# A gated long convolution beside a SiLU feed-forward on one core: another order of the seven products, constant matmuls at the start, an earlier load of S2, and a last product in two halves

## The chip, the core and the metric

The kernel runs on one core of a Trainium2 chip. The core has a matrix engine (TensorE, PE in the profile; its weight loads are PEld), VectorE (DVE), ScalarE (ACT), GpSimd (POOL) and a queue engine, SyncE (SP), from which most DMAs are issued; POOL issues the DMAs that add into DRAM. The metric is device microseconds of one execution; smaller is better. The profile's span runs from the first to the last instruction of the program.

## What is computed

```
xn = layernorm(q)                                   # q, k, v: 2048 x 1024
A:  k_shift = causal depthwise conv of k, 4 taps
    kv = k_shift * v
    y  = causal depthwise conv of kv with ssm_k (2048 taps, by FFT) + kv * ssm_D
    A  = xn * y
B:  h  = silu(xn @ w1)                              # w1: 1024 x 3584
    B  = h @ w2                                     # w2: 3584 x 1024
out = q + A + B
```

Everything is float32 outside; each matrix operand is held as a high and a low half in 16-bit floats, and a product is three matmuls (high·high, low·high, high·low).

## The kernel before

**The work.** It is one long stream on TensorE. The first GEMM (xn @ w1) has 14 pairs of 128-column blocks of w1. Pairs 0 and 1 of the first half of the rows run plainly (`plain_unit`, L951). All others run as *units* (`units`, L982): a two-by-two block product by seven products of sums instead of eight, named P1 to P7 in `PRODUCTS`, each of 12 matmuls of 512 columns. The left factors (A11, A12, A22, S1 to S4) are sums of transposed rows of xn and lie in eight big SBUF tiles, `places`; `XPLACE` says which. The right factors (B11, T2, T3, B21, B22, T1, T4) are sums of blocks of w1 and lie in the ring `wo`. There are 26 units: 12 for the first half of the rows (sp 0), 14 for the second (sp 1). The second GEMM (h @ w2) runs plainly for most of the hidden columns (`feed_forward`, L1031), over column halves h, rows of 128 t and chunks c of w2; rows in one entry of `TOGETHER` share a pass over the chunks. For eight hidden blocks (`PAIRS`) it runs by the same seven products in eight units (`units2`, L1092). Between these, the convolution (`convolution`, L1350) goes on mainly on VectorE, and its matmuls (L1520 to L1522 and L1711 to L1713) are put in between those of the GEMMs.

**A unit.** It holds three of the four PSUM banks of the ring `ff`: `one` (P1, then P2 added), `two` (a copy of P1, to which P6, P5 and P3 are added) and `c` (P7, then P4 added). The order on TensorE is P7, P6, P2, P5, then P1 of the *next* unit, then P3 and P4. `evacuate` (L909) is a stream of its own on ScalarE and VectorE: copy `one` into `two` after P1 (`seen["P1"]`, for which P6 waits); copy `two` to `u` after P6 (P5 waits for it); after P5 copy `two` to `d` (P3 waits for it); add `c` and `d` (P4 waits for it); SiLU of the sums. `evacuate2` (L1139) does the same in units2, with `a` in place of `u`, and its results are stored by POOL with an adding DMA (`G`), two of them through `copied`. Where a store is to be added to the last row block, the last unit first loads conv's part (`o`), adds it, and stores by SP (`L`). Buffers of these results come from `hfs`, six halves; `hts` holds the 16-bit halves of h and, later, parts of the convolution.

**The order of everything.** A planner (`Order`, L118) writes the order out when the program is built: each stream is a generator that yields operations (`Op`, with engine, reckoned duration, what it reads and writes) or waits for tokens; the planner always emits the operation with the smallest reckoned start less the stream's bias. The chip then runs each engine's instructions in that order, with semaphores in between. A change of an order or of a duration so re-plans all streams.

**The loads of the second half.** `load_x` (L1019) loads the seven sums of the second half from DRAM with transposing DMAs on SP, in the order of `PRODUCTS` (A11, S3, S2, A12, S1, S4, A22), each when the same place's sum of the first half has had its last use. Place 4 holds A21 first and then, as `room` (L861) says, the `parts` of the hidden quads in both halves; the chunks of w2 and the factors of units2 later take the places in the order of `W2PLACE` and `FPLACE`.

**The start.** `warm_up` (L1785) runs 22 matmuls of constants, 128x128 in float32 (two instructions each); the rows of x are then normalised, transposed on TensorE (L598) and split.

Of the kernel before, what the change touches and what calls it, by code (L numbers as in the profile page):

```python
# [11 lines left out]
F32 = mybir.dt.float32  # L12
# [6 lines left out]
ADD, SUB, MUL = ALU.add, ALU.subtract, ALU.mult  # L19

P = 128
# [96 lines left out]
class Order:  # L118
# [182 lines left out]
def h3_ffn_kernel(ctx, tc, x, kp, vs, fs, shift, dskip, w1, w2, cfwd, cinv, out):  # L301
# [559 lines left out]
    def room():  # L861

        for sp in range(2):
            yield flag["room", sp]
            yield places[4].ready
            t, tok = places[4].tile([P, 2, 2 * W], F32)
            parts.open(t, 2)
            yield flag["quads", sp]
            tok.set()
# [36 lines left out]
            add(blocks(i, b, hf, tok, (made,)), EB)  # L906
        return hf, made

    def evacuate(i, b, one, c, made, seen):  # L909

        yield ff.ready
        seen["bank"] = two, k2 = ff.tile([P, 4, P])
        yield a_act(two, one[0], AF.Copy)
        seen["P1"].set()
        yield vs_r.ready
        u, ut = vs_r.tile([P, 4, P])
        yield made["P6"]
# [9 lines left out]
        seen["P5"].set()  # L927
        low, done = yield from places_of(i, b + 1)
# [10 lines left out]
        add(silu(i, low, low, None, done), EB)  # L939

    def steps(o, w, xf, first, last, more=False):

# [39 lines left out]
    def units():  # L982

        todo = [(i, sp) for sp in range(2) for i in UNITS[sp]]
        yield ff.ready
        one = ff.tile([P, 4, P])
        yield from product("P1", *todo[0], one[0], True)
        for n, (i, sp) in enumerate(todo):
            if sp == 1:
                flag["unit", n - len(UNITS[0])].set()  # L990
                flag["room", 1].set()
            if i in PAIRS:
                add(quad(i, sp), 0.1)
            made, seen = defaultdict(Token), defaultdict(Token)
            yield ff.ready
            c = ff.tile([P, 4, P])
            add(evacuate(i, 2 * sp, one, c, made, seen), EB)
            yield from product("P7", i, sp, c[0], True)
            yield seen["P1"]
            two = seen["bank"][0]  # L1000
            yield from product("P6", i, sp, two)
            made["P6"].set()
            yield from product("P2", i, sp, one[0])
            made["P2"].set()
            yield seen["P6"]
            yield from product("P5", i, sp, two)
            made["P5"].set()
            if n + 1 < len(todo):
                yield ff.ready
                one = ff.tile([P, 4, P])  # L1010
# [5 lines left out]
            yield from product("P4", i, sp, c[0])  # L1016
# [14 lines left out]
    def feed_forward():  # L1031
# [13 lines left out]
        for h in range(2):  # L1045
            for ts in TOGETHER[h]:
# [17 lines left out]
        yield from units2()  # L1064


    TOGETHER = ([range(2)] + [(t,) for t in range(2, NT)],
                [(t,) for t in range(NT - 3)] + [range(NT - 3, NT)])

    def steps2(po, hx, wc, first, last, more=False):  # L1070
        for n in range(4):
            def mm(n=n):
                kw = dict(skip_group_check=more)
                nc.tensor.matmul(po, hx[:, n, 0, :], wc[:, n, 0, :], start=first and n == 0, stop=False, **kw)  # L1074
                nc.tensor.matmul(po, hx[:, n, 0, :], wc[:, n, 1, :], start=False, stop=False, **kw)  # L1075
                nc.tensor.matmul(po, hx[:, n, 1, :], wc[:, n, 0, :], start=False, stop=last and n == 3, **kw)  # L1076
            yield T(mm, po, [hx[:, n], wc[:, n]], 3 * 0.2185)

    tiles2 = [(sp, q) for sp in range(2) for q in range(4)]

    def uses2():

        yield 0, "P1"
        for u in range(len(tiles2)):
            for n in ("P7", "P6", "P2", "P5"):
                yield u, n
            if u + 1 < len(tiles2):
                yield u + 1, "P1"
            yield u, "P3"
            yield u, "P4"  # L1090

    def units2():  # L1092

        def product2(n, u, o, first=False):
# [4 lines left out]
            yield from steps2(o, hx, wc, first, True, not first)  # L1099
            htok.set()  # L1100
            if u == len(tiles2) - 1:
                wtok.set()

        yield ff.ready
        one = ff.tile([P, W])
        yield from product2("P1", 0, one[0], True)
        for u in range(len(tiles2)):
            made, seen = defaultdict(Token), defaultdict(Token)
            yield ff.ready
            c = ff.tile([P, W])  # L1110
            add(evacuate2(u, one, c, made, seen), EB)
            yield from product2("P7", u, c[0], True)
# [4 lines left out]
            yield from product2("P2", u, one[0])  # L1117
            made["P2"].set()
            yield seen["P6"]
            yield from product2("P5", u, two)  # L1120
            made["P5"].set()
            if u + 1 < len(tiles2):
                yield ff.ready
                one = ff.tile([P, W])
                yield from product2("P1", u + 1, one[0], True)
# [4 lines left out]
            yield from product2("P4", u, c[0])  # L1130
            made["P4"].set()

    def at(u, r, h):

# [1 line left out]
        t = 4 * (2 * sp + r) + q  # L1136
        return orr[t // T2, t % T2, :, h * W:(h + 1) * W]

    def evacuate2(u, one, c, made, seen):  # L1139
# [17 lines left out]
        yield made["P6"]  # L1157
        yield a_act(a, two, AF.Copy, invc2[:, 0:1])
        seen["P6"].set()
        yield made["P2"]  # L1160
        add(copied(*one, at(u, 0, 0)), EB)
# [4 lines left out]
        seen["P5"].set()  # L1166
        yield v_stt(d, c[0], invc2[:, 0:1], d, MUL, ADD)
        seen["P7"].set()
        yield G(at(u, 1, 1), d)
# [10 lines left out]
        yield made["P4"]  # L1180
        yield v_stt(a, c[0], invc2[:, 0:1], a, MUL, ADD)
# [603 lines left out]
    def warm_up():  # L1785
# [68 lines left out]
```

## Time and profile before

| what | us |
|---|---|
| median of three runs | 1257.39 (1256.72 to 1257.83) |
| the profiled execution | 1258.14 |
| its span, first to last instruction | 1256.4 |
| VectorE busy / ScalarE busy / POOL busy | 1117.9 / 790.5 / 83.5 |
| mean granted clock of TensorE, share of full | 0.994 |

The profiled execution is 0.75 us above the median of the runs, and 1.7 us of it lie outside the span. In the rows below a time is from the start of the span; a line of the timeline has start, duration, engine, line, operation, output and inputs, shapes, count, and in brackets how long the engine stood idle before it and what ended the wait. The records of successive matmuls overlap, so TensorE's pace is read from their starts or from their number in a window, not from their durations.

### The profile page before, as it was taken

The page shows a single profiled execution, that of the slowest core. Times are in us where ns is not written, and L with a number is a line of the kernel's source. Part 1 is how long each engine was busy: PE and PEld are TensorE (multiplying, and loading weights), DVE is VectorE, ACT ScalarE, POOL GpSimd, SP SyncE. Part 2 cuts the span into 40 slices and gives each one's busy share as a digit, 9 for nine tenths or more (in the row PEclk, how much of TensorE's full clock was granted, in tenths as well). Part 3 has the DMA queues.
Part 4 walks back from the last instruction along what each step waited for, and adds up shares of the span by engine and source line. Part 5 has one row for each costly group of instructions (what it writes and reads, how often), then busy time and mean ns, then how long its engine had stood idle before and what let it go on. Part 6 is the DMA issues. An engine that isn't in the chain of part 4 may idle for free. (4 is left out here: it accounts for less than half of the span.)

```text
span 1256.4 us, 17146 instructions
## 1 busy us (share of the span) xinstructions
PE 1232.6 (98%) x6034; PEld 597.5 (48%) x6034; DVE 1117.9 (89%) x1359; ACT 790.5 (63%) x1431; POOL 83.5 (7%) x93
## 2 busy tenths in 40 slices
PE   7999999999999999999999999999999999999996
PEld 6554444444444544444444544544544544454452
DVE  7999987997999789998999899799989889988970
ACT  7868888886588878568654643744653545563351
POOL 0000000000000000000000000000120030123132
PEclk8999999999999999999999999999999999999999
DMA  9276989989799899769984655688595497969765
GB/s 367 82 262 239 315 288 303 300 240 227 232 336 270 242 309 313 207 191 297 311 278 125 206 179 132 185 269 231 107 257 153 106 225 217 243 137 161 164 121 80
DMA packets 272662, 279.83 MB, mean 223 GB/s; under 512 B 73792, under 2 KB 192576, under 8 KB 271296
## 3 DMA queue, kind: packets, MB, share of 16 engines
q1 hardware_dynamic: 256848, 262.22, 67.9%
q0 software_dynamic: 15728, 16.52, 9.9%
q8 instruction: 47, 0.77, 0.3%
q14 instruction: 39, 0.32, 0.1%
HBM read 175.66 MB, written 88.34 MB: 210 GB/s over the span
## 5 line engine op out<-in xcount | busy, mean ns | idle before, releaser
L1074 PE MATMUL ff<-x,wo 128*128 128x512 f16 x864 | 327.9, 380 | 3.4 <-ACT hf L360 3.4
L1076 PE MATMUL ff<-x,wo 128*128 128x512 f16 x864 | 328.1, 380 | 0.0
L1075 PE MATMUL ff<-x,wo 128*128 128x512 f16 x864 | 327.9, 380 | 0.1
L946 PE MATMUL ff<-x,wo 128*128 128x512 f16 (+1 forms) x808 | 304.5, 377 | 6.2 <-ACT hf L360 3.0
L948 PE MATMUL ff<-x,wo 128*128 128x512 f16 (+1 forms) x808 | 304.8, 377 | 1.0 <-DVE wo L352 1.0
L947 PE MATMUL ff<-x,wo 128*128 128x512 f16 (+1 forms) x808 | 304.8, 377 | 0.0
L349 DVE TENSOR_TENSOR spec<-spec 128x512 f32<-128x512 f32 (+2 forms) x256 | 261.8, 1053 | 2.0
L1075 PEld LDWEIGHTS <-wo 128*128 128x128 f16 x864 | 84.6, 98 | 104.0 <-issue 4.7
L1076 PEld LDWEIGHTS <-wo 128*128 128x128 f16 x864 | 84.6, 98 | 102.6 <-issue 1.0
L1074 PEld LDWEIGHTS <-wo 128*128 128x128 f16 x864 | 85.5, 99 | 100.1 <-issue 0.6
L948 PEld LDWEIGHTS <-wo 128*128 128x128 f16 x808 | 79.6, 98 | 94.3 <-DVE wo L352 1.5
L947 PEld LDWEIGHTS <-wo 128*128 128x128 f16 x808 | 79.5, 98 | 93.8 <-issue 5.8
L946 PEld LDWEIGHTS <-wo 128*128 128x128 f16 x808 | 81.0, 100 | 90.2 <-ACT wo L360 1.7
L349 DVE TENSOR_TENSOR tmp<-spec 128x2048 f32<-128x2048 f32 (+1 forms) x48 | 92.7, 1933 | 0.9
L352 DVE SCALAR_TENSOR_TENSOR ht<-hf,wsc,ht 128x1024 f16<-128x1024 f32 (+1 forms) x56 | 67.4, 1203 | 7.5 <-ACT ht L360 7.2
L360 ACT ACTIVATE spec<-ps 128x512 f32<-128x512 f32 x92 | 53.2, 592 | 28.7 <-PE ps L1522 28.0
L352 DVE SCALAR_TENSOR_TENSOR wo<-raw,wsc,wo 128x512 f16<-128x512 f32 (+1 forms) x56 | 56.4, 1012 | 11.9 <-ACT wo L360 11.9
L346 POOL DMA_DIRECT2D out<-hf x47 | 45.8, 981 | 303.9 <-ACT hf L360 254.4
L360 ACT ACTIVATE hf<-ff,invc 128x512 f32<-128x512 f32 x32 | 21.9, 684 | 65.7 <-PE ff L1076 47.6
L360 ACT ACTIVATE ht<-hf,wsc 128x1024 f16<-128x1024 f32 (+1 forms) x56 | 60.8, 1085 | 3.4 <-DVE hf L349 2.1
L360 ACT ACTIVATE spec<-spec 128x1024 bf16<-128x1024 f32 x32 | 33.7, 1054 | 46.1 <-DVE spec L349 46.0
L349 DVE TENSOR_TENSOR spec<-tmp 128x512 f32<-128x512 f32 (+1 forms) x80 | 61.3, 792 | 0.7
(188 smaller groups left out, 1779.3 us busy)
## 6 DMA issues: line engine op xcount, KB each, us to landing
wo<-hs SPq DMA_DIRECT2D x160, 256.0 KB, 3.2
hs<-ht SPq DMA_DIRECT2D x80, 256.0 KB, 4.8
raw<-in_w SPq DMA_DIRECT2D x28, 512.0 KB, 5.9
wraw<-in_w SPq DMA_DIRECT2D x24, 512.0 KB, 5.4
w2n<-in_w SPq DMA_DIRECT2D x24, 512.0 KB, 6.1
out<-hf POOLq DMA_DIRECT2D x47, 256.0 KB, 4.5
kin<-in_kp SPq DMA_DIRECT2D x16, 704.0 KB, 5.1
xt<-in_x SPq DMA_DIRECT2D x16, 512.0 KB, 7.3
```

The costliest lines, as they stand in the source:

```text
L346: return Op("POOL", 1.1, 3.0, lambda: nc.gpsimd.dma_start(o, i, accum_op=ADD), [i], [o], m, 2.3 * n)
L349: return V(lambda: nc.vector.tensor_tensor(o, a, b, op=op), o, [a, b], **k)
L352: return V(lambda: nc.vector.scalar_tensor_tensor(o, a, s, b, op0=op0, op1=op1), o, [a, b] + ([] if isinstance(s, float) else [s]), **k)
L360: nc.scalar.activation(o, i, func, scale=scale, **kw)
L946: nc.tensor.matmul(o, w[:, 0, k], xf[:, :, k, 0], start=first and k == 0, stop=False, **kw)
L947: nc.tensor.matmul(o, w[:, 0, k], xf[:, :, k, 1], start=False, stop=False, **kw)
L948: nc.tensor.matmul(o, w[:, 1, k], xf[:, :, k, 0], start=False, stop=last and k == KH - 1, **kw)
L1074: nc.tensor.matmul(po, hx[:, n, 0, :], wc[:, n, 0, :], start=first and n == 0, stop=False, **kw)
L1075: nc.tensor.matmul(po, hx[:, n, 0, :], wc[:, n, 1, :], start=False, stop=False, **kw)
L1076: nc.tensor.matmul(po, hx[:, n, 1, :], wc[:, n, 0, :], start=False, stop=last and n == 3, **kw)
```

## The change

It has five parts.

1. In every unit but the first of `units` and the first of `units2` the products run P6, P7, P5, P2, next P1, P3, P4. With P1 the new `start` adds the unit's evacuation at once, ahead of the taking of a bank for `c`, which is taken when P7 begins. In `evacuate` the SiLU of P2's sum, and the buffer for it, come after P5's copy; the add of `c` and `d` is yielded only when P2 has been issued. In `evacuate2` P2's result is copied after the add of `c` and `d`.
2. `keep_warm` is a new stream with a bias of –0.3: wherever the planner would leave TensorE waiting by more than that, it puts constant matmuls of a reckoned 0.22 us, until row 3 of A12 is transposed. It holds one bank of `ff` so long.
3. `load_x` begins with S2, into place 4; the parts of the second half go to S2's old place. `W2PLACE` and `FPLACE` are rearranged.
4. The first pass of the second GEMM takes three row blocks together in place of two.
5. In the very last unit P4 runs by column halves, and each half is evacuated and stored by SP when it is done; P2's and P3's results and the buffer for conv's part may take a half of `hts`.

The diff, cut to its core:

```diff
-W2PLACE = [(2, 7, 6, 3, 4), (0, 1, 5, 2, 7)]
-FPLACE = (6, 3, 4, 0, 1, 5, 2, 7)
+W2PLACE = [(2, 4, 7, 0, 3), (1, 5, 6, 2, 4)]
+FPLACE = (7, 0, 3, 1, 5, 6, 2, 4)
...
-            yield places[4].ready
-            t, tok = places[4].tile([P, 2, 2 * W], F32)
+            r = places[(4, XPLACE["S2"])[sp]]
+            yield r.ready
+            t, tok = r.tile([P, 2, 2 * W], F32)
...
-    def evacuate(i, b, one, c, made, seen):
+    def evacuate(i, b, one, made, seen, early):
...
-        yield made["P2"]
-        up, both = yield from places_of(i, b)
-        add(silu(i, up[:, 0], *one, both), EB)
+        if early:
+            yield made["P2"]
+            yield from first()
         yield ws_r.ready
         d, dt = ws_r.tile([P, 4, P])
         yield made["P5"]
         yield a_act(d, two, AF.Copy)
         seen["P5"].set()
+        c = seen["c"]
+        if not early:
+            yield made["P2"]
+            yield from first()
...
+        def start(n):
+            i, sp = todo[n]
+            yield ff.ready
+            one = ff.tile([P, 4, P])
+            yield from product("P1", i, sp, one[0], True)
+            made, seen = defaultdict(Token), defaultdict(Token)
+            add(evacuate(i, 2 * sp, one, made, seen, n == 0), EB)
+            return one, made, seen
...
+            if n == 0:
+                yield from seventh()
             yield seen["P1"]
             two = seen["bank"][0]
             yield from product("P6", i, sp, two)
             made["P6"].set()
-            yield from product("P2", i, sp, one[0])
-            made["P2"].set()
+            yield from second() if n == 0 else seventh()
             yield seen["P6"]
             yield from product("P5", i, sp, two)
             made["P5"].set()
+            if n > 0:
+                yield from second()
             if n + 1 < len(todo):
-                yield ff.ready
-                one = ff.tile([P, 4, P])
-                yield from product("P1", *todo[n + 1], one[0], True)
+                following = yield from start(n + 1)
             yield seen["P5"]
             yield from product("P3", i, sp, two)
...
-        for name in [p[0] for p in PRODUCTS.values()]:
-            r = places[XPLACE[name]]
+        for name in ("S2", "A11", "S3", "S1", "A12", "S4", "A22"):
+            r = places[4 if name == "S2" else XPLACE[name]]
...
-    TOGETHER = ([range(2)] + [(t,) for t in range(2, NT)],
+    TOGETHER = ([range(3)] + [(t,) for t in range(3, NT)],
...
-            for n in ("P7", "P6", "P2", "P5"):
+            for n in ("P7", "P6", "P2", "P5") if u == 0 else ("P6", "P7", "P5", "P2"):
...
+            for q in range(2):
+                yield from product2("P4", u, seen["c"][0], cols=slice(q * W // 2, (q + 1) * W // 2), end=q == 1)
+                made["P4", q].set()
...
         def copied(src, tok, to):
-            yield hfs.ready
-            o, otok = hfs.tile([P, W])
+            yield lambda: hfs.ready() or last and hts.ready()
+            o, otok = (hfs if hfs.ready() else hts).tile([P, W])
...
         seen["P7"].set()
+        if u > 0:
+            yield made["P2"]
+            add(copied(*one, at(u, 0, 0)), EB)
         yield G(at(u, 1, 1), d)
         dt.set()
         if last:
             yield flag["conv out"]
-            yield hfs.ready
-            o, otok = hfs.tile([P, W])
+            yield lambda: hfs.ready() or hts.ready()
+            o, otok = (hfs if hfs.ready() else hts).tile([P, W])
...
+        for q in range(2):
+            yield made["P4", q]
+            cols = slice(q * W // 2, (q + 1) * W // 2)
+            yield v_stt(a[:, cols], c[0][:, cols], invc2[:, 0:1], a[:, cols], MUL, ADD)
+            yield L(at(u, 1, 0)[:, cols], a[:, cols])
         c[1].set()
-        yield L(at(u, 1, 0), a) if last else G(at(u, 1, 0), a)
         at_.set()
...
+    def keep_warm():
+
+        pt, tok = ff.tile([P, 4, P])
+        while not flag["turned", "A12", 3]():
+            yield T(lambda: nc.tensor.matmul(pt[:, 0, :], ones, ones, start=True, stop=True), pt[:, 0, :], [], 0.22)
+        tok.set()
...
+    add(keep_warm(), -0.3)
```

More of the change, by code (lines that the diff above doesn't have):

```diff
@@ L919, in evacuate, with first @@
         seen["P6"].set()
-        yield made["P2"]
-        up, both = yield from places_of(i, b)
-        add(silu(i, up[:, 0], *one, both), EB)
+        def first():
+            up, both = quads_up[i, b] = yield from places_of(i, b)
+            add(silu(i, up[:, 0], *one, both), EB)
+        if early:
+            yield made["P2"]
+            yield from first()
         yield ws_r.ready
@@ L939, in evacuate @@
         add(silu(i, low, low, None, done), EB)
+    quads_up = {}
     def steps(o, w, xf, first, last, more=False):
@@ L993, in units, with seventh, second @@
                 add(quad(i, sp), 0.1)
[L994 to L998, printed above, removed]
+            one, made, seen = following
+            def seventh():
+                yield ff.ready
+                seen["c"] = c = ff.tile([P, 4, P])
+                yield from product("P7", i, sp, c[0], True)
+            def second():
+                yield from product("P2", i, sp, one[0])
+                made["P2"].set()
+            if n == 0:
+                yield from seventh()
             yield seen["P1"]
@@ L1092, in units2, with product2 @@
     def units2():
-        def product2(n, u, o, first=False):
+        def product2(n, u, o, first=False, cols=slice(0, W), end=True):
             yield flag["h2", u, n]
@@ L1098, in product2, with start, seventh, second @@
             wc, wtok = w2f[n]
[L1099 to L1106, printed above, removed]
-        for u in range(len(tiles2)):
[L1108 to L1112, printed above, removed]
+            yield from steps2(o[:, cols], hx, wc[:, :, :, cols], first, True, not first)
+            if end:
+                htok.set()
+                if u == len(tiles2) - 1:
+                    wtok.set()
+        def start(u):
+            yield ff.ready
+            one = ff.tile([P, W])
+            yield from product2("P1", u, one[0], True)
+            made, seen = defaultdict(Token), defaultdict(Token)
+            add(evacuate2(u, one, made, seen), EB)
+            return one, made, seen
+        following = yield from start(0)
+        for u in range(len(tiles2)):
+            one, made, seen = following
+            def seventh():
+                yield ff.ready
+                seen["c"] = c = ff.tile([P, W])
+                yield from product2("P7", u, c[0], True)
+            def second():
+                yield from product2("P2", u, one[0])
+                made["P2"].set()
+            if u == 0:
+                yield from seventh()
             yield seen["P1"]
@@ L1116, in units2 @@
             made["P6"].set()
-            yield from product2("P2", u, one[0])
-            made["P2"].set()
+            yield from second() if u == 0 else seventh()
             yield seen["P6"]
@@ L1121, in units2 @@
             made["P5"].set()
+            if u > 0:
+                yield from second()
             if u + 1 < len(tiles2):
-                yield ff.ready
-                one = ff.tile([P, W])
-                yield from product2("P1", u + 1, one[0], True)
+                following = yield from start(u + 1)
             yield seen["P5"]
@@ L1166, in evacuate2 @@
         seen["P5"].set()
+        c = seen["c"]
         yield v_stt(d, c[0], invc2[:, 0:1], d, MUL, ADD)
         seen["P7"].set()
+        if u > 0:
+            yield made["P2"]
+            add(copied(*one, at(u, 0, 0)), EB)
         yield G(at(u, 1, 1), d)
```

29 lines of the change are left out of this document (17 added, 12 removed).

## The prediction

> **What bounds the kernel now.** I read the page's first two parts, then the matrix engine's waits. Columns of the waits: who waited for whom, microseconds in all, times, longest.
> ```profile
> span 1256.4 us, 17146 instructions
> ...
> PE 1232.6 (98%) x6034; PEld 597.5 (48%) x6034; DVE 1117.9 (89%) x1359; ACT 790.5 (63%) x1431; POOL 83.5 (7%) x93
> ...
> PE   7999999999999999999999999999999999999996
> ```
> ```profile
> PE ff L1074 <- ACT hf L360: 3.4, 2, 2.7
> PE ff L946 <- ACT hf L360: 3.0, 1, 3.0
> ...
> PE ff L946 <- DVE hf L349: 1.8, 1, 1.8
> ```
> The kernel is bound by TensorE: 98% busy, full in every slice but the first and the last. The change takes no product away, so it can only win what lies in the 24 us between 1232.6 and 1256.4, and in stretches where the clock is low. Two waits for ScalarE (3.0 in the FFN units, 3.4 in units2) and one for VectorE (1.8) are nearly all that is between the ends. VectorE at 89% is the next bound.
>
> The clock is read from windows laid on its changes. Columns: length, PE busy (x instructions), PEld, DVE, ACT, POOL, granted clock, DMA share, GB/s.
> ```profile
> 7.96:11.37 3.41, 1.48 (x14) 1.51 (x14) 2.61 (x6) 2.88 (x9) 0.00 (x0) 1.00 1.04 401
> 11.37:14.78 3.41, 1.09 (x9) 0.59 (x7) 3.23 (x12) 3.17 (x8) 0.00 (x0) 1.00 1.08 408
> 14.78:18.20 3.42, 2.45 (x12) 1.51 (x12) 3.42 (x8) 3.37 (x9) 0.00 (x0) 0.50 1.03 420
> 18.20:21.61 3.41, 3.41 (x18) 2.54 (x17) 3.27 (x10) 2.80 (x7) 0.00 (x0) 0.50 1.02 408
> 21.61:25.02 3.41, 3.41 (x33) 3.19 (x32) 1.62 (x5) 1.78 (x4) 0.00 (x0) 1.00 1.04 409
> ...
> 584.81:588.22 3.41, 0.45 (x4) 0.10 (x2) 2.77 (x5) 3.31 (x8) 0.00 (x0) 1.00 1.15 343
> 588.22:591.63 3.41, 3.41 (x10) 1.21 (x9) 3.38 (x4) 1.86 (x6) 0.00 (x0) 0.50 1.06 324
> ...
> 1236.76:1240.17 3.41, 1.14 (x6) 0.55 (x6) 0.00 (x0) 0.69 (x1) 0.00 (x0) 1.00 0.73 105
> 1240.17:1243.58 3.41, 3.06 (x8) 0.94 (x7) 0.00 (x0) 1.00 (x2) 0.86 (x1) 0.50 0.24 20
> ```
> Each window with 1.14 us or less of PE work in 3.41 is followed by half clock; the one with 1.48 is not. So a stall costs twice: itself, then half of what the next 3.41 us could do, up to 1.7 us.
>
> **Term A: constant matmuls at the start.**
> ```profile
> 16.07 0.40 PE L948 MATMUL ff<-x,wo 128*128 128x256 f16 x1 [0.97 <-DVE wo L352]
> ...
> 17.13 0.73 DVE L352 SCALAR_TENSOR_TENSOR wo<-x,wsc,wo 128x512 f16<-128x512 f32 x1
> ...
> 21.92 0.23 DVE L733 TENSOR_SCALAR wsc<-powers,pow 128x3 f32<-128x3 f32 x1
> ...
> 22.60 1.47 PE L598 MATMUL ft<-ident,xt 128*128 128x128 f32 x12
> ...
> 23.87 1.89 DVE L352 SCALAR_TENSOR_TENSOR x<-ft,x 128x512 f16<-128x512 f32 x3 [1.72 <-ACT x L360]
> ```
> keep_warm puts matmuls of constants into the waits ahead of the first products. The first products run at half clock until 21.61: 18 matmuls in a window where the next has 33. If the fillers raise the window 11.37–14.78 above 1.48, that goes. Not all is won, since the parts of W1 arrive when they arrive. At full clock a group of 12 takes 12 x 3.41/33 = 1.24 us. Group one runs from 16.07 to 17.3, group two waits for the part ready at 17.13 + 0.73 = 17.86, so groups two and three end at 20.3 where now they end at 22.60. The next rows' transposes come some 2 us earlier; their three splits on VectorE, now from 23.87 after 1.72 idle, can start when it comes free at 21.92 + 0.23 = 22.15, which is 1.7 earlier. From there both engines shift together. **A = 1.6**, between 0 (the clock falls all the same) and 3.4 (half of two windows). Fillers delay nothing if they stand only in reckoned waits; the PSUM bank they hold is given back when row 3 is transposed, ahead of the second unit.
>
> The Trainium skill, "TensorE: Matmul & The Clock Gate", section "Part 1: The HAM clock gate (the "warmup" mystery)", has the clock fall after at least one idle window of about 3.4 us. Here it fell after windows that held 0.45, 1.09 and 1.14 us of work, so the trace disagrees. By that rule B and C below would have no half-clock share, and the sum would be some 3 us smaller.
>
> **Term B: the last FFN unit.** Order before: P7, P6, P2, P5, next P1, P3, P4; the last unit has no next P1, so P3 follows P5 at once and waits for ScalarE's copy of P5's bank.
> ```profile
> 584.66 0.38 PE L948 MATMUL ff<-x,wo 128*128 128x512 f16 x1
> ...
> 587.37 0.58 ACT L360 ACTIVATE hf<-ff 128x512 f32<-128x512 f32 x1
> ```
> ```profile
> 588.00 0.40 PE L946 MATMUL ff<-x,wo 128*128 128x512 f16 x1 [2.96 <-ACT hf L360]
> ```
> ```profile
> 1244.00 0.38 PE L1074 MATMUL ff<-x,wo 128*128 128x512 f16 x1 [0.78 <-ACT hf L360]
> ...
> 1248.96 0.38 PE L1076 MATMUL ff<-x,wo 128*128 128x512 f16 x1
> ```
> Between 1244.00 and 1248.96 lie 23 steps of 0.216, so a product of 12 is 2.59 us. After the change P2 stands between P5 and P3 and covers 2.59 of the 588.00 – 584.66 – 0.22 = 3.12 lost; 0.53 is left, no window falls below 1.48, and the half-clock window (1.7) goes. **B = 3.12 + 1.7 – 0.53 = 4.3.** Upper end 4.8. Lower end 0, if ScalarE is later still by that much: its copy was itself held up by loads and conv work.
>
> **Term C: stalls of the last unit of units2.**
> ```profile
> 1226.05 0.69 ACT L360 ACTIVATE hf<-ff,invc 128x512 f32<-128x512 f32 x1 [3.62 <-PE ff L1076]
> ```
> ```profile
> 1234.09 1.77 POOL L346 DMA_DIRECT2D out<-hf  x2 [2.91 <-issue]
> ...
> 1235.99 0.38 PE L1076 MATMUL ff<-x,wo 128*128 128x512 f16 x1
> 1238.29 0.69 ACT L360 ACTIVATE hf<-ff,invc 128x512 f32<-128x512 f32 x1 [10.94 <-DMA out<-hf]
> 1239.03 0.38 PE L1074 MATMUL ff<-x,wo 128*128 128x512 f16 x1 [2.66 <-ACT hf L360]
> ...
> 1248.84 0.69 DVE L349 TENSOR_TENSOR hf<-hf 128x512 f32<-128x512 f32 x1 [4.11 <-DMA hf<-out]
> ...
> 1249.62 0.69 ACT L360 ACTIVATE hf<-ff,invc 128x512 f32<-128x512 f32 x1 [5.67 <-DVE hf L349]
> 1249.64 0.75 DVE L352 SCALAR_TENSOR_TENSOR hf<-ff,invc,hf 128x512 f32<-128x512 f32 x1
> 1250.42 0.34 SPq L336 DMA_DIRECT2D out<-hf  x1
> 1250.61 0.86 POOL L346 DMA_DIRECT2D out<-hf  x1 [4.60 <-ACT hf L360]
> ...
> DMA to landing us min/median/max: 2.0/4.1/5.7
> ```
> P3's wait at 1244.00 goes, with P2 between: 0.8, and its half-clock part makes it **1.2**. P5's wait at 1239.03 is another kind: the copy of P6 (1238.29) waited for a store out of its buffer. That store is the one of 1234.09, of what was copied at 1226.05, just ahead of this unit's first copy. The wait is 1239.03 – 1235.99 – 0.22 = 2.82, and with 1.2 of half clock 4.0. After the change the unit's first copy is issued right behind its P1, ahead of the previous unit's P3, so its buffer can only be one stored a product or two earlier; but P5 comes one product earlier too (P6, P7, P5). Upper end 4.0; lower end –2.6, if the landing stays where it is. I take **2.3**, nearer the upper end, because the late store can no longer be the buffer's last user.
>
> **Term D: the tail.** From the last matmul's start (1248.96) to the end of the last store (1250.61 + the median 4.1 = 1254.7) are 5.7 us; the span closes 1.7 later, as before. That store carries P3's bank: its copy (1249.62) waited for the buffer into which conv's part was read back, which was landed and added only at 1248.84 + 0.69. Now a free ht buffer may serve, so the copy starts when P3 ends, and the read-back on SP stands behind d's store as before, with all of P3 and P4 to land. Two halves of P4 are 24 matmuls at 3.41/33 = 0.10, as long as 12 at 0.216. P3's store lands at –2.6 + 0.4 + 0.7 + 0.3 + 4.1 = 2.9 after the last matmul's start; the second half of P4 at 0.3 + 0.4 (half of the 0.75) + 0.1 + 2.0 = 2.8. **D = 5.7 – 2.9 = 2.8**, between 1.0 (POOL's queue, which now takes d, P2's and P3's results within five us, is late by 1.8) and 3.2.
>
> **Term E: the early S2.** load_x is one sequence on SP's queue. Now S2 goes first, into place 4, which the last quad must free; A11 stands behind it, and the first P1 of the second half needs A11.
> ```profile
> L342 SPq DMA_TRANSPOSE x<-xspA x3: 4722/4793/4934, 273.7 to 309.7; - x3
> ...
> L352 DVE SCALAR_TENSOR_TENSOR ht<-x,wsc,ht x1: 1276/1276/1276, 273.1 to 273.1; 128x1024 f16<-128x1024 f32 x1
> ...
> DMA to landing us min/median/max: 6.8/7.4/9.2
> ```
> Place 4 is read until 273.1 + 1.3 = 274.4; S2's issue takes 4.8; A11 lands at 274.4 + 4.8 + 7.4 = 286.6, against 273.7 + 7.4 = 281.1 now. P1 of that unit stands behind four products with conv matmuls between, which can fill. **E = –0.5**, from 0 to –3.5 (landing 9.2, no conv to fill).
>
> **Term F: seams elsewhere.** P1 to P6 loses a product of cover (P3, P4, P7 becomes P3, P4, 5.2 us); P5 to P3 gains one; P6 to P5 keeps one. VectorE's add for P7 is now issued behind P2, and P4 waits for it over P1 and P3 as before; behind it on VectorE stand splits and conv. The written order re-plans every conv step. The 1.8 for VectorE may go or move. Bounds: +2 (it goes) and –13 (four stalls as dear as 588's with half clock would be 19, as dear as the plain ones 7; I take the middle). I take **–2**, near the plain row of 1.8. The places' new order follows the order in which products release them; the three rows at GEMM2's start give each chunk of W2 one product more cover: nothing.
>
> **Sum:** 1.6 + 4.3 + 1.2 + 2.3 + 2.8 – 0.5 – 2 = 9.7. The profiled execution took 1258.1 (span 1256.4 and 1.7 around it), so 1248.4; the median shown, 1257.4, is 0.7 under it, so **1247.7**.
>
> **Rivals.**
> 1. The fillers don't hold the clock (the planner sees too few waits): A = 0, **1249.3**, chance 0.15. For: it reckons 0.44 for each warm-up matmul, and those ended early. Against: 0.4 us more work lifts the window above 1.48. The Trainium skill, "TensorE: Matmul & The Clock Gate", section "Part 4: PE-mode transpose", says that transposes do not count as busy for the gate; then the window would need more fillers. Against that stands 7.96–11.37: nearly all of its 1.48 are transposes, and the next window has full clock.
> 2. The last unit's buffer still lands late and P5 comes a product sooner: C's second part –2.6 in place of 2.3, **1252.6**, chance 0.15. For: the 7 us between 1226.05 + 0.69 and the store's issue at 1234.09 are POOL's queue, which the change leaves full.
> 3. Seams give it back: two stalls like 588's (9.4), **1257**, chance 0.12: VectorE at 89% has little room when TensorE gains.
> 4. Slower: P1 to P6, at 5.2 us of cover. Where ScalarE also serves conv (290 to 597) it was behind by 587.37 – 584.88 = 2.5 us once; a silu and a copy must fit. Each miss costs 1.9 to 4.8; against the 11.7 gained without F it decides from about four misses on: **1261**, chance 0.16. Against: no wait of that place is among the rows.
>
> **How the numbers follow.** My forecast has 0.42. A measurement tells about 0.2% (2.5 us) from no change. Faster: 0.42 + 0.15 + 0.15 = 0.72; same 0.12; slower 0.16. The range, 1240 to 1258.5, reaches down to A, B, C and D at their upper ends less 2, and up over rival 3; it leaves out rival 4 and little below.
>
> **What would show it.** Right: no window at half clock between 14 and 22; no wait of P3 for ScalarE's copy of P5 in either last unit; last store landed about 2.9 after the last matmul's start. Wrong: new waits of PE for ACT or DVE at the head of a unit (P6), a gap in PE near 285 for A11, or P5 of the last unit still behind a store.

## The result and the profile after

The changed kernel takes 1257.55 us in the median of 12 runs (1253.22 to 1261.77); the kernel before took 1256.64 beside it (12 runs, 1254.72 to 1257.83). The ratio is 1.0004, with a 95% interval of 0.9992 to 1.0016: no difference. Forecast was 1247.7. The profiled execution of the changed kernel took 1256.67, of which 2.27 lie outside its span (before: 1.7). One execution among the runs below, of a_tail2, took 1685 us at a granted clock of 0.72 and is left out of that run's median and ratio.

The page's first parts, for the changed kernel:
```profile
span 1254.4 us, 17286 instructions
...
PE 1233.2 (98%) x6092; PEld 602.1 (48%) x6092; DVE 1116.4 (89%) x1360; ACT 788.5 (63%) x1431; POOL 83.4 (7%) x93
...
PE   9999999999999999999999999999999999999997
```
The first slice is full now, and the last one is at 7 tenths where it was at 6. The windows at the start (columns as in the prediction: length, PE, PEld, DVE, ACT, POOL, granted clock, DMA share, GB/s) and the last row transposes ahead of the first whole products:
```profile
11.37:14.78 3.41, 3.31 (x30) 3.13 (x29) 3.24 (x12) 3.16 (x8) 0.00 (x0) 1.00 1.07 403
14.78:18.20 3.42, 3.42 (x33) 3.20 (x32) 3.42 (x8) 3.39 (x9) 0.00 (x0) 1.00 1.03 414
18.20:21.61 3.41, 3.41 (x34) 3.19 (x33) 3.27 (x10) 3.26 (x8) 0.00 (x0) 1.00 1.04 418
```
```profile
42.74 1.82 PE L598 MATMUL ft<-ident,xt 128*128 128x128 f32 x12 [0.34 <-DVE x L352]
```
The same line in the kernel before:
```profile
44.65 1.82 PE L598 MATMUL ft<-ident,xt 128*128 128x128 f32 x12 [0.34 <-DVE x L352]
```
The constant matmuls keep the clock at full speed, and all that follows comes 1.91 us earlier: term A is there (1.6 was forecast). The waits of TensorE for others in the changed kernel (us in all, times, longest):
```profile
PE ff L958 <- ACT hf L360: 3.9, 4, 2.3
PE ps L1578 <- ACT tmp L360: 3.2, 2, 2.3
...
PE py L491 <- ACT spec L360: 0.6, 1, 0.6
```
The wait of the last FFN unit, both waits of units2's last unit and the 1.8 for VectorE are gone; in their place stand four waits of other FFN units for a copy by ScalarE and four of conv's matmuls (`ps`, `py`; the fourth, 0.4, for VectorE), which waited once before, for 0.6.

The head of P3 in the last FFN unit (its first matmul is the last line):
```profile
590.47 0.38 PE L960 MATMUL ff<-x,wo 128*128 128x512 f16 x1
590.90 0.38 PE L958 MATMUL ff<-x,wo 128*128 128x512 f16 x1
```
It loses 590.90 – 590.47 – 0.22 = 0.2 us, where it lost 3.1 and then 1.7 in a window of half clock: term B is 4.6 (4.3). The last unit of units2, from P5's copy to the end:
```profile
1237.82 0.69 ACT L360 ACTIVATE hf<-ff,invc 128x512 f32<-128x512 f32 x1 [4.64 <-DMA out<-hf]
...
1239.71 0.86 POOL L346 DMA_DIRECT2D out<-hf  x1 [6.24 <-DVE hf L352]
...
1243.81 0.33 SPq L336 DMA_DIRECT2D hf<-out  x1
...
1245.16 0.27 PE L1102 MATMUL ff<-x,wo 128*128 128x256 f16 x1
1247.08 0.69 DVE L349 TENSOR_TENSOR hf<-hf 128x512 f32<-128x512 f32 x1 [7.79 <-DMA hf<-out]
1247.86 0.69 ACT L360 ACTIVATE hf<-ff,invc 128x512 f32<-128x512 f32 x1 [6.91 <-DVE hf L349]
...
1248.39 0.81 SPq L336 DMA_DIRECT2D out<-hf  x2
1248.90 0.86 POOL L346 DMA_DIRECT2D out<-hf  x1 [6.78 <-ACT hf L360]
```
TensorE waits for nothing here (term C is 2.82 + 1.2 + 0.8 + 0.4 = 5.2, where 3.5 was forecast). P5's copy (1237.82) still stood behind a store out of its buffer, as its row says, but it starts 0.35 us after P5's end (last matmul at 1237.25, plus 0.22), and P2 covers that. TensorE starts its last matmul at 1245.16, 3.8 earlier than before. But the span ends 9.24 after that, not 7.44. The read-back of conv's part (1243.81) is issued 4.1 us after the store of P5's result (1239.71), and all behind it waits for it: the addition, the copy of P3's bank, the last store.

So the account of the two profiled executions is: start 1.9, last FFN unit 4.6, last unit of units2 5.2, together 11.7; but the last matmul is only 3.8 earlier, so **7.9 are lost between**; the tail loses 1.8 and what lies outside the span 0.5. That leaves 1.5 (1258.14 – 1256.67); the medians, which differ by nothing, lie 1 us above the one trace of the changed kernel and 1.5 under that of the kernel before. The 7.9 can also be added up from the trace: what the spacings of successive matmul starts have over 0.216 (512 columns; 0.109 for 256) comes to 9.9 us between 47 and 1245, against 12.1 before, of which B and C were 10.0. This sum is called the stream's loss below.

### The profile page after: what moved, and what is told of

The parts are those of the page before. It is cut to its first block, busy times and chain, and to the rows that moved or that the text cites. A ratio compares the mean times of both kernels' runs of the same rounds, so it can differ in the third digit from the quotient of the medians.

```text
span 1254.4 us, 17286 instructions
## 1 busy us (share of the span) xinstructions
PE 1233.2 (98%) x6092; PEld 602.1 (48%) x6092; DVE 1116.4 (89%) x1360; ACT 788.5 (63%) x1431; POOL 83.4 (7%) x93
## 4 chain that ended last, share of the span: by engine, by line
PE 72%; DVE 11%; DMA 7%; ACT 6%; issue 3%; SPq 0%; POOLq 0%; POOL 0%; DVEq 0%; ACTq 0%
PE ff L1100 12%; PE ff L1101 12%; PE ff L1102 12%; PE ff L958 9%; PE ff L959 9%; PE ff L960 9%; DVE spec L349 4%; DMA w2n<-in_w 2%; PE ps L1578 2%; DVE tmp L349 2%; PE ps L1580 2%; PE ps L1579 2%; DMA lo<-cm 1%; DVE x L352 1%; ACT hf L360 1%
## 5 line engine op out<-in xcount | busy, mean ns | idle before, releaser
L352 DVE SCALAR_TENSOR_TENSOR acc<-kin,taps,acc 128x1024 f32<-128x1024 f32 x48 | 61.5, 1281 | 1.5 <-ACT acc L360 1.5
```

Source lines behind the costliest of these rows:

```text
L352: return V(lambda: nc.vector.scalar_tensor_tensor(o, a, s, b, op0=op0, op1=op1), o, [a, b] + ([] if isinstance(s, float) else [s]), **k)
```

## Experiments

Two theories on the 7.9 us. **T2**, which I favoured: the new order puts P6 right behind the previous unit's P4, so ScalarE's copy of P6, for which P5 waits, stands in its queue behind that unit's SiLUs and splits. **T1**: VectorE is nearly as full as TensorE in the middle, with ScalarE in step with it, so time gained by TensorE comes back as waits, whatever the order. Columns as before, the changed kernel by stage:
```profile
290.00:600.00 310.00, 305.59 (x1469) 143.57 (x1468) 280.11 (x321) 235.43 (x411) 2.27 (x3) 1.00 0.87 261
600.00:900.00 300.00, 297.09 (x1444) 141.30 (x1443) 280.60 (x297) 153.14 (x307) 4.99 (x6) 1.00 0.69 208
900.00:1080.00 180.00, 179.96 (x874) 85.47 (x873) 167.21 (x184) 94.07 (x196) 29.29 (x30) 1.00 0.79 192
```
VectorE is busy 90, 94 and 93% there (the 99% of the first expectation below is too high). For T2 speaks the largest of the FFN units' waits; the rows are TensorE's last matmul of P6 and first of P5, and ScalarE's queue:
```profile
511.79 0.38 PE L960 MATMUL ff<-x,wo 128*128 128x512 f16 x1
514.50 0.38 PE L958 MATMUL ff<-x,wo 128*128 128x512 f16 x1 [2.33 <-ACT hf L360]
```
```profile
507.52 0.72 ACT L360 ACTIVATE cm<-acc,csc 128x512 f16<-128x512 f32 x1 [5.03 <-DMA lo<-cm]
508.15 0.67 ACT L360 ACTIVATE x<-ff,wsc 128x512 f32<-128x512 f32 x1
508.85 1.15 ACT L360 ACTIVATE ht<-x,wsc 128x1024 f16<-128x1024 f32 x1
...
512.06 1.15 ACT L360 ACTIVATE hf<-hf,wsc 128x1024 f32<-128x1024 f32 x1 [0.41 <-DVE hf L349]
513.24 0.72 ACT L360 ACTIVATE ht<-hf,wsc 128x512 f16<-128x512 f32 x1
513.87 0.58 ACT L360 ACTIVATE hf<-ff 128x512 f32<-128x512 f32 x1
```
The bank is complete at 511.79 + 0.22, the copy (513.87) starts 1.9 later, behind a SiLU (512.06) and a split. In the mean over the 26 units this lag, from the start of P6's last matmul plus 0.216 to the copy, is 1.53 us in the changed kernel and 0.45 in the kernel before.

Times are medians of 4 to 12 executions; the ratio is to the kernel before on the same chip (1256.3 to 1257.1 in all four groups).

| run | us | ratio (95%) |
|---|---|---|
| b_warm | 1252.76 | 0.9973 (0.9962 to 0.9984) |
| a_nowarm | 1255.31 | 0.9995 (0.9983 to 1.0007) |
| a_oldunits | 1250.29 | 0.9949 (0.9936 to 0.9961) |
| a_tail | 1251.34 | 0.9959 (0.9946 to 0.9972) |
| after2 | 1258.10 | 1.0016 (1.0003 to 1.0030) |
| a_ulow | 1255.88 | 0.9993 (0.9981 to 1.0006) |
| a_old_tail | 1248.87 | 0.9937 (0.9919 to 0.9954) |
| a_old2_tail | 1249.94 | 0.9949 (0.9932 to 0.9965) |
| a_oldunits2 | 1251.51 | 0.9960 (0.9945 to 0.9975) |
| a_old_tail2 | 1247.78 | 0.9928 (0.9911 to 0.9945) |
| b_warm_tail | 1250.96 | 0.9952 (0.9936 to 0.9968) |
| a_old_tail_whole | 1246.55 | 0.9918 (0.9901 to 0.9934) |
| a_tail2 | 1252.86 | 0.9968 (0.9958 to 0.9978) |
| a_ulow_tail | 1251.01 | 0.9955 (0.9942 to 0.9968) |
| best_nowarm | 1250.58 | 0.9947 (0.9936 to 0.9959) |
| best_lateS2 | 1248.47 | 0.9934 (0.9923 to 0.9946) |

The traces show which pairs have one order: where only the last unit's buffers differ, or only the halves of the last P4, or only the constant matmuls, TensorE, ScalarE and VectorE keep the order of all other instructions. Every other edit lets the planner rearrange conv's steps, so a part of its difference is the new plan.

### The constant matmuls

b_warm is the kernel before with this line and `keep_warm`; a_nowarm is the changed kernel without the line.
```diff
+    add(keep_warm(), -0.3)
```


> The kernel before with the constant matmuls ahead of the first products added, and nothing else. Theory T2 (the new order of the units loses time by itself, because ScalarE's copy of P6 now queues behind the previous unit's SiLUs): with the old order the start's gain has nobody to eat it, so 1.5 to 2 us less than before, about 1255. Theory T1 (VectorE, busy over 99% between 290 and 900, sets the pace in the middle, whatever the order): the first products end 1.9 us earlier, but new waits of TensorE for VectorE or ScalarE give it back by the start of the second GEMM, so 1256.6, the time of before, within 0.5.

> The changed kernel without the constant matmuls ahead of the first products. T2: the waits of P5 for the copy of P6 stay (some 4 us over the FFN's units), and the start's loss of 1.9 us is seen in full: about 1259.4. T1: the units begin 1.9 us later, the side engines are less behind, so some 2 us of TensorE's waits in the middle go: 1257.5, as the changed kernel.

In the old order they are worth 3.7 us (1252.76 against 1256.46), which T1 doesn't allow and which is more than the 1.9 of the start: in the profiled execution the stall at 585 is there with 2.67, but without the half clock behind it. In the new order they are worth nothing: a_nowarm is not slower than the changed kernel but 1 to 2.6 us faster by the ratios (the intervals overlap), as T1 has it. Since the orders are the same, this is no new plan: in a_nowarm's trace the row transposes shown above begin 1.73 us later (44.47), and the stream's loss behind them is 5.6 us where it is 9.9 and, in after2, 8.6. Neither theory holds alone.

### The order of the FFN units

```diff
-            add(evacuate(i, 2 * sp, one, made, seen, n == 0), EB)
+            add(evacuate(i, 2 * sp, one, made, seen, n + 1 < len(todo)), EB)
...
-            if n == 0:
+            if n + 1 < len(todo):
                 yield from seventh()
...
-            yield from second() if n == 0 else seventh()
+            yield from second() if n + 1 < len(todo) else seventh()
...
-            if n > 0:
+            if n + 1 == len(todo):
                 yield from second()
```


> The changed kernel with the order of before (P7, P6, P2, P5) in all units of the first GEMM pair but the last one; the second GEMM's order, the constant matmuls, the early S2 and the halves of the last P4 stay. T2: the lag from the end of P6 to the start of its copy falls from 1.5 us in the mean back to about 0.45, P5's waits for it go, and the time is 5 to 7 us under the changed kernel, about 1251. T1: the waits move to another product, or to the conv matmuls, and the time is 1256 to 1258.

> The changed kernel once more, beside the other three on the same chip, since single runs of it lay between 1253.2 and 1261.8. Both theories: 1257.5, within 1; the waits of P5 for the copy of P6 of units 12 to 23 are there again, some 3 to 5 us together, though not in the same units.

> The kernel with the old order in the first GEMM pair's units but the last, once more, beside the same with the other buffers, on one chip: the first time the two were 1.4 us apart (1250.29 and 1248.87) where the traces' tails differ by 4.3. If the tail's gain holds here too, this run is 3 to 5 us above the next one, near 1251; if not, within 2 us of it.

With the old order in all units but the last the kernel takes 1250.29 and 1251.51, where the changed kernel takes 1257.55 and 1258.10: about 7 us. The mean lag of the copy is 0.61 and 0.65. (after2 shows how much single traces differ: its FFN units wait once, for 1.5, where the first trace has 3.9.) The waits that are left, in a_oldunits2:
```profile
PE ff L958 <- ACT hf L360: 2.1, 2, 1.8
...
PE ps L1578 <- ACT tmp L360: 0.8, 1, 0.8
```
The 1.8 is the same P5 as at 514 above, and the order isn't its cause: ScalarE, which keeps its order, stood 3.47 us ahead of conv's `cm` for a transposing load, and the copy behind it.
```profile
512.72 0.72 ACT L360 ACTIVATE cm<-acc,csc 128x512 f16<-128x512 f32 x1 [3.47 <-DMA lo<-cm]
...
514.39 0.57 ACT L360 ACTIVATE hf<-ff 128x512 f32<-128x512 f32 x1
```

### The SiLU ahead of the copy

The new order stays; only the SiLU of a unit's low pair waits for the next unit's copy of P6.
```diff
...
+        if gate is not None:
+            yield gate
         yield a_act(o, src, AF.Silu, wsc[:, i, 3:4])
...
+        flag["u copied", n].set()
...
-        add(silu(i, low, low, None, done), EB)
+        add(silu(i, low, low, None, done, flag["u copied", n + 1] if n < 25 else None), EB)
```


> The changed kernel with its new order, in which only the SiLU of a unit's low pair (behind P4) is issued on ScalarE behind the next unit's copy of P6. T2 (the copy stands in ScalarE's queue behind that SiLU): the mean lag from P6's end to its copy falls from 1.5 us to under 0.8, P5's waits of units 12 to 23 mostly go, and the time is 3 to 5 us under the changed kernel, about 1253.5. T1 (VectorE sets the pace, the order doesn't matter): the waits come back at other products or at the conv matmuls, 1256 to 1258.

> The changed kernel with the last unit's buffers from the other pool, once more, as the base for the next one: 1251 to 1252.5.

> The same with the SiLU of a unit's low pair issued behind the next unit's copy of P6. T2 alone: all that the old order gains comes from ScalarE's queue at that place, so this one reaches the old order with these buffers: 1248 to 1249. T1 beside it: only a part comes back (without these buffers it was 2 us) and the rest is waits of TensorE in other places: 1250 to 1251.

The lag falls to 0.66 (0.57 in a_ulow_tail), and in a_ulow one wait of 0.1 is left of the FFN units' 3.9. Yet the time falls by 2.2 us only (1255.88 against 1258.10), and with the other buffers of the next section by 1.9 (1251.01 against 1252.86), in both pairs with overlapping intervals, where the old order brings about 7 and about 4 (2.5 and 5.1 in its two pairs). The waits of a_ulow:
```profile
PE ff L1107 <- DVE x L352: 1.9, 1, 1.9
...
PE ff L1106 <- ACT ff L360: 1.3, 1, 1.3
PE ps L1584 <- ACT tmp L360: 1.2, 1, 1.2
...
PE ff L1106 <- ACT x L360: 0.7, 1, 0.7
```
TensorE now waits in the second GEMM, between 1075 and 1096: for operands (`x`, 1.9 and 0.7), which VectorE and ScalarE make beside conv, and for a copy of P1 (`ff`, 1.3). The trace of a_ulow_tail has waits in the same place, the longest (2.3) followed by a window of half clock. **T2 as the only cause falls.** It accounts for about 2 us of the 4 to 7. That the rest is T1 is not shown, for conv's plan is another one too. The single traces speak for a larger part: the stream's loss is 8.6 to 14.3 us (11.4 in the mean) in the four traces of the new order with the constant matmuls, 6.2 and 8.5 with this SiLU moved, and 2.3 to 8.0 (5.7 in the mean) in the eight with the old order in all FFN units but the last. But a trace is one execution: that of a_ulow took 1253.14, 2.7 less than its median and no more than that of a_oldunits (1253.39).

### The tail's buffers

TensorE's order is that of the changed kernel.
```diff
-            o, otok = (hfs if hfs.ready() else hts).tile([P, W])
+            o, otok = (hts if last and hts.ready() else hfs).tile([P, W])
...
-            o, otok = (hfs if hfs.ready() else hts).tile([P, W])
+            o, otok = (hts if hts.ready() else hfs).tile([P, W])
             yield L(o, at(u, 1, 0))
```


> The changed kernel, in which in the last unit the buffer for the read-back of conv's part and those of the copies of P2 and P3 are taken from the other pool (ht) first, so that the read-back needn't wait for the store of P5's result. TensorE's order is the same. Tail theory (the end is a chain of latencies: store of d, read-back into the same half, add, copy of P3 into that half again, store): the read-back is issued about 4 us sooner, P3's copy starts when P3 ends, and the last store lands 3 to 4 us earlier: about 1254. Rival (the last stores wait for POOL's queue or for the DMA engines, not for the buffer): within 0.5 us of the changed kernel.

> The old order in all units of the first GEMM pair but the last, and the last unit's buffers from the other pool. If the two are independent, both gains add: 1250.3 less the tail's 4.3 (tail of 4.93 us in the trace of the run with the other buffers against 9.24) is 1246. If the tail's gain comes only where TensorE runs late (the store that it waits for is then already landed), it is 1249 to 1250.

> The best so far, once more, on the same chip as the one before: 1247 to 1249 by either reading; what is told apart is its distance from the one before.

> The kernel before with the constant matmuls and the last unit's buffers from the other pool; TensorE's order and all the rest as before. Tail theory: the store, read-back, add, copy and store stand in the kernel before as well, so the buffers alone give 2 to 4 us on the 1252.8 with the constant matmuls: 1249 to 1251. If it is as fast as the kernel with the last units' new order (1248.9), the new order of the last units, the early S2 and the halves are worth nothing beside the buffers; by the trace they should be worth 3 to 5 us (the waits at 585, 1233 and 1236 with the constant matmuls: 2.67, 1.78 and 0.78).

a_tail is 6.2 us faster than the changed kernel, a_tail2 5.2 than after2. With the old order the buffers bring 1.4 in the first pair and 3.7 in the second (1251.51 and 1247.78); in b_warm_tail 1.8, or 2.6 by the ratios. The end of a_old_tail2:
```profile
1231.94 0.75 DVE L352 SCALAR_TENSOR_TENSOR hf<-ff,invc,hf 128x512 f32<-128x512 f32 x1 [9.58 <-ACT hf L360]
...
1232.61 0.68 DVE L349 TENSOR_TENSOR hf<-hf,ht 128x512 f32<-128x512 f32 x1
...
1234.75 0.69 ACT L360 ACTIVATE ht<-ff,invc 128x512 f32<-128x512 f32 x1 [2.09 <-PE ff L1102]
...
1235.73 0.86 POOL L346 DMA_DIRECT2D out<-ht  x1 [0.86 <-ACT ht L360]
...
1237.06 0.27 PE L1102 MATMUL ff<-x,wo 128*128 128x256 f16 x1
1237.37 0.88 DVE L352 SCALAR_TENSOR_TENSOR hf<-ff,invc,hf 128x256 f32<-128x256 f32 x2 [4.08 <-PE ff L1102]
1237.88 0.89 SPq L336 DMA_DIRECT2D out<-hf  x2
```
Conv's part has long been read back (the addition of 1232.61 waits for nothing), P3's copy starts when P3 ends, and its store is issued ahead of the last matmul. From the last matmul to the span's end are 5.9 us here and 4.6 to 5.9 in all ten traces with these buffers, against 8.8 to 10.3 in seven with the others (those of the changed and edited kernels). The tail theory holds.

b_warm, whose tail nobody edited, has 8.8 where the kernel before has 7.4: its last unit has no window of half clock, so its last matmul comes earlier against the same chain of stores.

### The rest

In a_old2_tail the second GEMM's units but the last have the old order too; a_old_tail_whole has the old order in the FFN units, the other buffers and the last P4 whole; best_nowarm and best_lateS2 are that kernel without the constant matmuls, and with `load_x`, `room`, `W2PLACE` and `FPLACE` of before.
```diff
...
-            for n in ("P7", "P6", "P2", "P5") if u == 0 else ("P6", "P7", "P5", "P2"):
+            for n in ("P7", "P6", "P2", "P5") if u + 1 < len(tiles2) else ("P6", "P7", "P5", "P2"):
...
```
```diff
...
-        for q in range(2):
-            yield made["P4", q]
...
-            yield L(at(u, 1, 0)[:, cols], a[:, cols])
+        yield made["P4"]
+        yield v_stt(a, c[0], invc2[:, 0:1], a, MUL, ADD)
+        yield L(at(u, 1, 0), a)
```


> As the one before, with the order of before in the second GEMM's units too, except the last. T2 for the second GEMM: there ScalarE is busy only some 40 to 60% and no SiLU stands in its queue, so the order is worth nothing: within 1 us of the one before. Rival: the waits of P6's product and of the conv matmuls in that stretch (0.7 at 1084, 0.9 at 1124) come from the new order, 1 to 2 us less.

> As the best so far, with the very last P4 whole: one addition of 0.75 us and one store behind it, no halves. By the rows of the trace the halves take the first half's addition and store off the end: 0.3 to 0.5 us, which five rounds hardly tell from nothing. Rival (24 matmuls of half the width cost more than 12 whole ones, and a second store is issued at the end): within 0.5 us, or faster.

> The fastest so far (old order but in the last units, other buffers, last P4 whole; 1246.55) without the constant matmuls ahead of the first products. If the start's gain is kept to the end, as in the kernel before (3.7 us with them), 1.9 to 3.7 us more: 1248.5 to 1250. If it is given back in the middle (T1), within 0.7 us of 1246.55.

> The fastest so far with S2's load, its place and the places of W2 as before. By the prediction's term E the early S2 costs 0.5 us, so 1246; by the trace of the changed kernel, which shows no wait of TensorE between 119 and 323, it is worth nothing either way: 1246 to 1247. If S2's late load held up a product, over 1248.

The second GEMM's order makes no difference that can be told (1249.94 and 1248.87). The halves of the last P4 gain nothing: whole it is 1.2 us faster (1246.55 and 1247.78, intervals overlapping), and the tail is 5.7 against 5.7 and 5.9. Without the constant matmuls this kernel takes 4.0 us more, about as in the old order. Without the early S2 it takes 1.9 more, with overlapping intervals: a small gain or none, not a cost. The time is over the 1248 that was to mean a product held up by S2's late load, but the trace has no wait for a load there: between 270 and 330 TensorE waits once, 0.3 us, for VectorE.

**a_old_tail_whole is the fastest, 1246.55 us**: 10.6 under the kernel before on the same chip, and below the changed kernel. It keeps the constant matmuls, the early S2, the pass of three row blocks and the new order in the last FFN unit and in the second GEMM's units; it drops the new order in the other FFN units and the halves. It is 4.4 us faster than b_warm_tail on that chip (1250.96). What of this is the last units' order, the early S2 or the other plan of conv, no run separates.

## Why the prediction was wrong

- **The frame held.** TensorE is the bound at 98%, and what can be won is in stalls, low clock and the ends. The clock rule read from the windows held in each new case.
- **A, B and C were right in mechanism**, and in size too, or too small: 1.9 for 1.6, 4.6 for 4.3, 5.2 for 3.5. C came out at its upper end, 1.2 + 4.0: all of it went. The half-clock parts of B and C (1.7 and 1.6) hold for the one profiled execution of before: in b_warm's trace stalls of 2.67 and 1.8 at the same places brought no half clock.
- **E** was priced –0.5; the trace of the changed kernel shows no wait of TensorE between 119 and 323, so it is 0.
- **D failed, by 4.6 us** (+2.8 forecast, –1.8 measured). The step that failed is "now a free ht buffer may serve, so the copy starts when P3 ends". The code asks hfs first, and the planner counts a half as free once the store out of it stands in the order. So the read-back got the half that held P5's result, and on the chip waited for that store (1239.71 to 1243.81) before it could begin; P3's copy then took that half again. I had read "may" as "does". I had also left out that C's stalls covered a part of this chain. The forecast's sign, the last store landed 2.9 us after the last matmul's start, came out as 7.8 (1248.90 and 4.1 to landing, against 1245.16).
- **F failed, by 5.9 us** (–2 forecast, –7.9 in the trace). The step is "P6 to P5 keeps one", of products of cover. The cover is kept, but what stands in ScalarE's queue ahead of the copy is not the same: P6 now follows P4, whose SiLU and splits come at that moment. I had counted products on TensorE and not instructions on the engine that has to answer. The upper end was there too, the 1.8 for VectorE went; so the other seams lost more than 9 us. The runs put 2 us on that, and 4 to 7 on the new order as a whole; where the rest comes from (T1's waits at other places, which a_nowarm shows with one and the same order, or the conv steps planned anew) no run separates, and it stays open.
- Another 0.5 us lies outside the span, the same in every run of the changed kernel (2.16 to 2.27; before 1.7 to 1.8). No run looked into it.
- Of the rivals the third came closest: the seams give the gain back, and the time is 1257. That its number fits is in part luck: it took 9.4 more off for the seams than the forecast, where the trace has 5.9, and D's failure, which was in no rival, made up for it.

## What to carry to other kernels

When an order is changed so that a consumer gets cover, go through the queue of each engine that answers and list what stands ahead of the answer at that moment; equal cover in products is not equal slack. A stall that is removed near the end uncovers the chain of stores behind it, so cost that chain from its own rows, with the buffers that the program really takes. And where the parts of a change are separable, run them apart: here the constant matmuls alone brought 3.7 us, and the change without the new order of most FFN units and the halves, with other buffers, was 10.6 us faster than the kernel before.

## What the runs showed of the hardware

**A stall of the same length costs nothing more or 1.7 us more, by where it falls.** The windows of 3.41 us follow one another without a gap from the start of the trace on; the wait of conv at 686 is 2.33 in the changed kernel and 2.32 in a_tail. In the changed kernel:
```profile
684.53:687.94 3.41, 1.49 (x7) 0.68 (x7) 3.41 (x4) 2.95 (x5) 0.00 (x0) 1.00 0.27 77
687.94:691.36 3.42, 3.42 (x26) 2.45 (x25) 2.37 (x4) 3.15 (x6) 0.00 (x0) 1.00 0.38 77
```
In a_tail, whose TensorE has the same instructions:
```profile
683.60:687.01 3.41, 1.09 (x6) 0.48 (x5) 3.41 (x4) 3.00 (x5) 0.00 (x0) 1.00 0.28 77
687.01:690.42 3.41, 3.41 (x14) 1.76 (x12) 2.85 (x4) 2.23 (x4) 0.00 (x0) 0.50 0.21 43
```
There the stall lies in one window, which has 1.09 us of work left, and the next one has half clock; in the other it lies across two. In a_oldunits 1.30 us of work in a window was followed by half clock as well:
```profile
511.80:515.22 3.42, 1.30 (x7) 0.49 (x6) 3.38 (x7) 3.38 (x6) 0.00 (x0) 1.00 1.08 394
515.22:518.63 3.41, 3.41 (x10) 1.21 (x9) 1.86 (x2) 0.68 (x2) 0.00 (x0) 0.50 0.83 282
```
So in these traces the border lies between 1.30 and 1.48. This can make executions of one kernel differ, for the phase of the windows is another in each: in a_tail2, which is a_tail's kernel once more, the stall near 686 is followed by full clock (1.86 us of work in its window), and one at 513, after which a_tail has full clock, by a window of half clock (1.31). The Trainium skill, "TensorE: Matmul & The Clock Gate", section "Part 1: The HAM clock gate (the "warmup" mystery)", calls the window free-running, and the traces agree.

**An adding store by POOL is slow to land.** At the end of the kernel before, where little else moves, its last store of 256 KB (1250.61) took 4.1 us to land, and the plain one of 256 KB by SP issued just before it (1250.42) took 2.0. Over the whole changed kernel, where a plain store shares the engines with other transfers, the medians lie closer (KB each, median us to landing; the last line are the two halves at the end):
```profile
out<-hf POOLq DMA_DIRECT2D x47, 256.0 KB, 4.9
...
out<-hf SPq DMA_DIRECT2D x16, 256.0 KB, 4.1
...
out<-hf SPq DMA_DIRECT2D x2, 128.0 KB, 1.7
```
Whether the adding or POOL's queue makes the difference, no run tells. A load into the half out of which such a store is read waits for the whole store, and then takes its own 3.3 (1243.81 to the addition at 1247.08). The Trainium skill, "DMA: Bandwidth & Descriptors", section "Anatomy of one DMA — SWDGE (gpsimd) path", gives 2.0 us and bytes/436e3, which for 256 KB is an estimate of 2.6; the adding stores here took 4.1 at the end of the kernel before and 4.9 in the median of the changed one.
